# Loading the first four input tiles as row pairs, and moving the V weights to another queue

## The chip, the cores and the metric

The kernel runs on one core of one Trainium2 chip. The metric is the device time of one execution in microseconds, lower is better. A profiled execution also leaves a trace of the instructions of each engine and of each DMA packet. The engines are named PE (TensorE, matrix multiplication), PEld (its weight load), DVE (VectorE), ACT (ScalarE), POOL (GpSimd) and SP (SyncE, which here only issues DMAs). SPq, ACTq and POOLq are the DMA issues of SP, ACT and POOL.

## The reference

The input x has 2048 tokens (rows) of 512 bf16 values. With `xn = layernorm(x)` (no learned scale), the output is `x + A(xn) + B(xn)`.

```python
def _layernorm(x, axis=-1, eps=1e-5):
    return (x - mean) / sqrt(var + eps)
# A: linear attention, 32 heads of 16
q, k, v = split(xn @ wqkv)
phi(t) = concat(softmax(t @ w_phi), softmax(-(t @ w_phi)))      # per head
kv = sum over tokens of phi(k)^T v ; z = sum over tokens of phi(k)
A = (phi(q) kv / (phi(q) z + 1e-6)) @ wo
# B: gated unit, inner width 1792
B = ((xn @ w_gate) * (xn @ w_up)) @ w_down
```

Every step but the sum over tokens in `kv` and `z` works on one token at a time, and that sum does not depend on the order of the tokens.

## The kernel before, in words

The tokens are cut into 16 tiles of 128 rows. `xall` holds all of x in SBUF, tile n at `xall[:, n, :]`, and partition p of tile n is row 128n + p. Four tiles are a group. `xnT` is the normalised x, transposed, so that it can be an operand of every projection.

PE, DVE, ACT, POOL and SP each run their instructions in the order in which the program writes them (`tc.manual_schedule`, line 87); an engine that waits holds up all that stands behind it on that engine.

The start of the program matters here:

- **Loads** (lines 82 to 103). SP issues x tile 0, x tile 2, the second half of `wv` (`dma_wv(2, DC)`, rows 256 to 511 of the V weights), then the first columns of `wg` and `wu`, then `wphi`, more of `wg` and `wu`, a transposing load of the K weights (`wT2`), x tiles 4 to 7, and so on. ACT issues x tile 1 and the first half of `wv`, behind the load of its function table and in front of its other work. POOL issues x tile 3.
- **Semaphores.** The loads by SP and ACT take turns on eight completion semaphores, so a load waits, on the queue that issues it, for the load that had its semaphore eight loads earlier. The load by POOL has a semaphore of its own.
- **Warm-up** (lines 305 to 315). Nine matmuls on constants run on PE while the first tile is under way.
- **First group** (lines 376 to 405). For tiles 0 to 3 the layer norm is folded in later: only the row sum is subtracted before the transposition. `sum_of(0)` sums tile 0 on DVE; ACT sums tiles 1 and 2 (`junk`, line 378, with an accumulated output `tot`); `sum_of(3)` is on DVE. `sub_sum(n)` (line 338, DVE) writes `xns[n]`, `lt(n)` (line 206, PE) transposes it into a PSUM bank and ACT or DVE copies it to `xnT` (line 207). `first_v(n, js)` multiplies `xnT` of tile n by chunks `js` of `wv`: chunks 0 and 1 are the first half, 2 and 3 the second. The order on PE is: tile 0 transposed, tile 1 transposed, `first_v(0, (0, 1))`, tile 2 transposed, `first_v(1, (0, 1))`, `first_v(2, (0, 1))`, `first_v(0, (2, 3))`, tile 3 transposed, and the rest.
- The order on DVE is: sum of tile 0, `sub_sum` of 0 in two halves, `sub_sum` of 1, two copies, `sub_sum` of 2, a copy, sum of tile 3, a copy, `sub_sum` of 3, then the statistics of the four tiles. The order on ACT is: the two sums, then three copies.

After that the program interleaves units of the gated unit (`ffn`, 8 matmuls each) with the projections of K, V and Q, the sums of `kv`, and, in its second half, attention and the output tiles (`fin`). `fin(n)` adds x and stores tile n from SP (line 302). At the end SP waits for the semaphores of all engines and DMAs, one after the other, and all engines meet in a barrier.

Of the kernel before, what the change touches and what calls it, by code (L numbers as in the profile page):

```python
# [21 lines left out]
def kernel(  # L22
# [12 lines left out]
    nc = tc.nc  # L35
    P = 128
# [4 lines left out]
    NT = S // P  # L41
    DC = D // P
# [4 lines left out]
    TT = GT * P  # L47
    E1 = DH + 1

    x_view = A_x.flatten_outer_dims().rearrange("(n p) d -> p n d", n=NT)  # L50
    out_view = out.flatten_outer_dims().rearrange("(n p) d -> p n d", n=NT)

    consts = ctx.enter_context(tc.tile_pool(name="consts", bufs=1))
    wpool = ctx.enter_context(tc.tile_pool(name="wpool", bufs=1))
# [2 lines left out]
    xall = xpool.tile([P, NT, D], BF16)  # L57
# [10 lines left out]
    def dma_x(lo, hi, eng=nc.sync):  # L68
        eng.dma_start(out=xall[:, lo:hi, :], in_=x_view[:, lo:hi, :])

    def dma_cols(eng, w, src, lo, hi, at=0):
        eng.dma_start(out=w[:, :, lo - at:hi - at], in_=src[:, lo:hi].rearrange("(c p) f -> p c f", p=P))

    def dma_wv(lo, hi, eng):
        eng.dma_start(out=wv[:, lo:hi, :],
                      in_=A_wqkv[lo * P:hi * P, 2 * D:3 * D].rearrange("(c p) f -> p c f", p=P))

    def dma_gu(lo, hi):
        dma_cols(nc.sync, wg, B_w_gate, lo, hi)
        dma_cols(nc.sync, wu, B_w_up, lo, hi)  # L80

    dma_x(0, 1)
    dma_x(2, 3)
    dma_wv(2, DC, nc.sync)

    ET = mybir.EngineType
    ctx.enter_context(tc.manual_schedule(engines={ET.PE, ET.DVE, ET.Activation, ET.Pool, ET.SP}))
    ones = nc.const_aps.tensor(1.0, [P, P], BF16)
    first = consts.tile([P, 1], BF16)
    nc.scalar.activation(out=first[:], in_=ones[:, 0:1], func=AF.Exp, scale=1.0)  # L90
    dma_x(1, 2, nc.scalar)
    dma_wv(0, 2, nc.scalar)
    dma_x(3, 4, nc.gpsimd)
    dma_gu(0, 2 * P)
    nc.sync.dma_start(out=wphi[:], in_=A_w_phi.rearrange("(c h) d f -> (h d) c f", c=DC))
    dma_gu(2 * P, 5 * P)
# [49 lines left out]
    def bank(name, dt=F32, n=TT):  # L146
        return ps_s.tile([P, n], dt, name=name, tag="s")
# [137 lines left out]
    def fin(n, cuts=(0, D)):  # L285
        T, t4 = n // GT, n % GT
        for lo, hi in zip(cuts, cuts[1:]):
            w = hi - lo
            ps = bank("fin")[:, 0:w]
            for f in range(FC):  # L290
                nc.tensor.matmul(ps, lhsT=hTs[T][:, f, t4 * P:(t4 + 1) * P], rhs=wd[:, f, lo:lo + w],  # L291
                                 start=(f == 0), stop=False)
            for c in range(DC):
                nc.tensor.matmul(ps, lhsT=oTs[n][:, c, :], rhs=wo[:, c, lo:lo + w],  # L294
                                 start=False, stop=(c == DC - 1))
            o_sb = opool.tile([P, w], BF16, name=f"o_sb{w}")
            if n < GT:
                nc.vector.scalar_tensor_tensor(out=o_sb[:], in0=ps, scalar=r2[n][:], in1=xall[:, n, lo:lo + w],
                                               op0=ALU.mult, op1=ALU.add)
            else:  # L300
                nc.vector.tensor_tensor(out=o_sb[:], in0=ps, in1=xall[:, n, lo:lo + w], op=ALU.add)  # L301
            nc.sync.dma_start(out=out_view[:, n, lo:lo + w], in_=o_sb[:])


    warm = bank("warm")
# [153 lines left out]
    with tc.tile_pool(name="ps_ab", bufs=1, space=PSUM) as ps_ab, \  # L459
# [23 lines left out]
        for n in range(NT):  # L483
            attend(n)
            if n + 5 < NT:
                qproj(n + 5)
            if n < 2:
                ffn(2)
                continue
            fin(n - 2)  # L490
            if n >= 4:
                ffn(2)
        ffn(len(units))
        fin(NT - 2)
        fin(NT - 1, (0, 3 * P, D))


# [28 lines left out]
```

## Time and profile before

| what | us |
|---|---|
| time, median of 3 runs | 220.43 (220.23 to 220.95) |
| time of the profiled execution | 220.46 |
| its span, first to last instruction | 218.8 |
| around the span | 1.66 |
| PE busy in the span | 214.9 |
| DVE busy | 141.0 |
| ACT busy | 89.2 |
| POOL busy | 74.9 |

The span is what the trace shows; 1.66 us of the time lie outside it. A view by line groups the instructions; a view in order of time shows the start, the duration, the engine, the line, the output tile and its input. "Idle before" is how long the engine had nothing to do before that instruction, and the arrow names what ended this.

### The profile page before, as it was taken

What the parts mean: (1) busy time and instruction counts of PE and PEld (TensorE: products, weight loads), DVE (VectorE), ACT (ScalarE), POOL (GpSimd) and SP (SyncE); (2) the same over time, 40 slices, a digit from 0 to 9 for tenths busy, and PEclk for the clock granted to TensorE, in tenths of its full rate; (3) what the DMA queues carried; (4) which work ended last, traced back from release to release, by engine and by line L of the source; (5) the groups of instructions that cost most, each with busy time, mean ns of one, the idle gap of its engine ahead of it and who ended that gap; (6) DMA issues with size and microseconds to landing.
All of it is one profiled execution on the core that took longest, in us unless ns stands there. A gap on an engine that the chain in (4) does not pass through costs nothing.

```text
span 218.8 us, 3493 instructions
## 1 busy us (share of the span) xinstructions
PE 214.9 (98%) x1291; PEld 103.1 (47%) x1291; DVE 141.0 (64%) x242; ACT 89.2 (41%) x159; POOL 74.9 (34%) x72
## 2 busy tenths in 40 slices
PE   8999999999999999999999999999999999999994
PEld 3444445454444444444544444444444444454443
DVE  4878867786598758576599773296655655454321
ACT  5545686569575875565435212141231322100000
POOL 4450843373357554636045333033123033000000
PEclk9999999999999999999999999999999999999999
DMA  5999996005202240202028355114461431412201
GB/s 198 286 297 372 372 219 136 2 0 51 48 0 49 51 94 2 48 3 48 1 43 105 76 114 114 37 24 96 96 70 30 95 72 28 96 48 72 69 30 48
DMA packets 48433, 19.91 MB, mean 91 GB/s; under 512 B 37504, under 2 KB 48384, under 8 KB 48416
## 3 DMA queue, kind: packets, MB, share of 16 engines
q1 hardware_dynamic: 47952, 19.16, 38.9%
q10 hardware_dynamic: 416, 0.39, 0.5%
q8 instruction: 10, 0.16, 0.3%
q0 software_dynamic: 48, 0.13, 0.2%
q14 instruction: 7, 0.06, 0.1%
HBM read 8.67 MB, written 2.10 MB: 49 GB/s over the span
## 4 chain that ended last, share of the span: by engine, by line
PE 97%; DMA 1%; DVE 1%; issue 0%
PE g L275 22%; PE fin L291 22%; PE u L279 22%; PE fin L294 6%; PE q L237 6%; PE k L237 6%; PE pv L237 6%; PE kv L331 2%; PE ab L465 2%; DMA xall<-in_A_x_dram 1%; PE kv L237 1%; PE tp L206 1%; PE pq L226 1%; DVE tot L374 0%; DVE xn L338 0%; DVE o_sb L301 0%
## 5 line engine op out<-in xcount | busy, mean ns | idle before, releaser
L275 PE MATMUL g<-xnT,wg 128*128 128x512 bf16 x224 | 57.5, 379 | 0.0
L279 PE MATMUL u<-xnT,wu 128*128 128x512 bf16 x224 | 57.5, 379 | 0.0
L254 POOL TENSOR_TENSOR phiq<-e,rsum 128x1024 bf16<-128x1024 f32 x16 | 30.9, 1933 | 63.5 <-DVE rsum L252 56.0
L283 DVE TENSOR_TENSOR hT<-u,g_sb 128x512 bf16<-128x512 f32 x56 | 37.0, 666 | 23.9 <-PE u L279 15.8
L282 ACT CAST g_sb<-g 128x512 bf16<-128x512 f32 x56 | 32.9, 587 | 46.8 <-PE g L275 46.5
L250 DVE TENSOR_REDUCE sums<-e 128x64 f32<-128x1024 f32 x32 | 38.9, 1216 | 20.1 <-ACT e L247 20.1
L291 PE MATMUL fin<-wd,hT 128*128 128x512 bf16 (+2 forms) x238 | 51.1, 366 | 0.0
L254 POOL TENSOR_TENSOR phik<-e,rsum 128x1024 bf16<-128x1024 f32 x16 | 30.9, 1932 | 39.6 <-DVE rsum L252 33.6
L279 PEld LDWEIGHTS <-wu 128*128 128x128 bf16 x224 | 21.9, 98 | 26.4
L291 PEld LDWEIGHTS <-hT 128*128 128x128 bf16 x238 | 22.4, 98 | 24.8
L275 PEld LDWEIGHTS <-wg 128*128 128x128 bf16 x224 | 21.1, 98 | 24.0
L237 PEld LDWEIGHTS <-xnT 128*128 128x128 bf16 x192 | 17.4, 98 | 18.2 <-ACT xnT L207 0.7
L301 DVE TENSOR_TENSOR o_sb<-fin,xall 128x512 bf16<-128x512 f32 (+2 forms) x13 | 8.5, 651 | 20.5 <-PE fin L294 20.5
L252 DVE RECIPROCAL rsum<-sums 128x64 f32<-128x64 f32 x32 | 17.7, 553 | 3.1
L294 PE MATMUL fin<-wo,oT 128*128 128x512 bf16 (+2 forms) x68 | 16.6, 366 | 0.0
L237 PE MATMUL k<-W1k,xnT 128*128 128x512 bf16 x64 | 16.4, 379 | 0.0
L237 PE MATMUL q<-W1q,xnT 128*128 128x512 bf16 x64 | 16.4, 378 | 0.0
L246 ACT ACTIVATE e<-q 128x512 f32<-128x512 f32 x12 | 7.2, 597 | 22.2 <-PE q L237 22.2
L237 PE MATMUL pv<-wv,xnT 128*128 128x512 bf16 x56 | 14.4, 379 | 0.0
L478 DVE TENSOR_TENSOR otok<-ab,rden 128x512 bf16<-128x512 f32 x16 | 11.1, 692 | 0.6
L323 ACT CAST vt<-pv 128x512 bf16<-128x512 f32 x12 | 7.0, 587 | 10.0 <-PE pv L237 10.0
L154 DVE BATCH_NORM_STATS2 stats<-xall 128x6 f32<-128x512 bf16 x16 | 10.6, 664 | 0.0
(63 smaller groups left out, 131.8 us busy)
## 6 DMA issues: line engine op xcount, KB each, us to landing
out_dram<-o_sb SPq DMA_DIRECT2D x15, 128.0 KB, 2.0
wd<-in_B_w_down_dram SPq DMA_DIRECT2D x1, 1792.0 KB, 15.8
xall<-in_A_x_dram SPq DMA_DIRECT2D x1, 1024.0 KB, 11.9
wg<-in_B_w_gate_dram SPq DMA_DIRECT2D x1, 640.0 KB, 7.7
wu<-in_B_w_up_dram SPq DMA_DIRECT2D x1, 640.0 KB, 10.4
xall<-in_A_x_dram SPq DMA_DIRECT2D x1, 512.0 KB, 4.5
wg<-in_B_w_gate_dram SPq DMA_DIRECT2D x1, 512.0 KB, 5.3
wu<-in_B_w_up_dram SPq DMA_DIRECT2D x1, 512.0 KB, 6.4
```

The lines of the kernel that those rows point to most:

```text
L154: nc.vector.bn_stats(out=stats[:], in_=xall[:, n, :])
L237: nc.tensor.matmul(ps, lhsT=xnT[:, j, n * P:(n + 1) * P], rhs=w[:, j, :], start=(j == 0), stop=(j == DC - 1))
L250: nc.vector.tensor_reduce(out=sums[:], in_=ev, axis=AX.X, op=ALU.add)
L252: nc.vector.reciprocal(out=rsum[:].rearrange("p a b -> p (a b)"), in_=sums[:])
L254: nc.gpsimd.tensor_tensor(out=phi[:].rearrange("p g (x f) -> p (g x) f", f=DH), in0=ev, in1=rsum[:].to_broadcast((P, 2 * H, DH)), op=ALU.mult)
L275: nc.tensor.matmul(gps, lhsT=wg[:, c, f * P:(f + 1) * P], rhs=xnT[:, c, T * TT:(T + 1) * TT], start=(c == 0), stop=(c == DC - 1))
L279: nc.tensor.matmul(ups, lhsT=wu[:, c, f * P:(f + 1) * P], rhs=xnT[:, c, T * TT:(T + 1) * TT], start=(c == 0), stop=(c == DC - 1))
L282: nc.scalar.copy(out=g_sb[:], in_=gps)
L283: nc.vector.tensor_tensor(out=hTs[T][:, f, :], in0=ups, in1=g_sb[:], op=ALU.mult)
L291: nc.tensor.matmul(ps, lhsT=hTs[T][:, f, t4 * P:(t4 + 1) * P], rhs=wd[:, f, lo:lo + w], start=(f == 0), stop=False)
L294: nc.tensor.matmul(ps, lhsT=oTs[n][:, c, :], rhs=wo[:, c, lo:lo + w], start=False, stop=(c == DC - 1))
L478: nc.vector.tensor_tensor(out=o_tok[:].rearrange("p (b h d) -> p b h d", b=2, d=DH), in0=abv[:, :, :, 0:DH], in1=rden[:].to_broadcast((P, ...
```

## The change

Tiles 0 and 1 become a pair, and tiles 2 and 3 as well. A pair is 256 consecutive rows of x. Partition p gets rows 2p and 2p + 1 of these 256, the first in the even tile's slot of `xall` and the second in the odd tile's slot. The two rows lie next to each other in memory and in the partition, so a pair is one load of 128 pieces of 2 KB, where there were two loads of 128 pieces of 1 KB each. Each of the four tiles then holds other rows than before, and the store of tiles 0 to 3 goes by the same map. SP issues both pairs; ACT issues the two halves of `wv`; POOL issues no load. There is one load less by SP and ACT, and one less by POOL.

```diff
+    PAIRS = (0, 2)
+    def pair(rows, n):
+        return rows[n * P:(n + 2) * P, :].rearrange("(p j) d -> p j d", j=2)
+    def out_of(n, lo, hi):
+        if n // 2 * 2 in PAIRS:
+            return pair(out_rows, n // 2 * 2)[:, n % 2, lo:hi]
+        return out_view[:, n, lo:hi]
...
+    def dma_pair(n, eng=nc.sync):
+        eng.dma_start(out=xall[:, n:n + 2, :], in_=pair(x_rows, n))
...
-    dma_x(0, 1)
-    dma_x(2, 3)
-    dma_wv(2, DC, nc.sync)
+    dma_pair(0)
+    dma_pair(2)
...
     nc.scalar.activation(out=first[:], in_=ones[:, 0:1], func=AF.Exp, scale=1.0)
-    dma_x(1, 2, nc.scalar)
     dma_wv(0, 2, nc.scalar)
-    dma_x(3, 4, nc.gpsimd)
+    dma_wv(2, DC, nc.scalar)
     dma_gu(0, 2 * P)
...
-            nc.sync.dma_start(out=out_view[:, n, lo:lo + w], in_=o_sb[:])
+            nc.sync.dma_start(out=out_of(n, lo, lo + w), in_=o_sb[:])
```

More of the change, by code (lines that the diff above doesn't have):

```diff
@@ L48 @@
     E1 = DH + 1
-    x_view = A_x.flatten_outer_dims().rearrange("(n p) d -> p n d", n=NT)
-    out_view = out.flatten_outer_dims().rearrange("(n p) d -> p n d", n=NT)
+    x_rows, out_rows = A_x.flatten_outer_dims(), out.flatten_outer_dims()
+    x_view = x_rows.rearrange("(n p) d -> p n d", n=NT)
+    out_view = out_rows.rearrange("(n p) d -> p n d", n=NT)
+    PAIRS = (0, 2)
[5 more added lines that the diff above has]
+        return out_view[:, n, lo:hi]
     consts = ctx.enter_context(tc.tile_pool(name="consts", bufs=1))
```

## The prediction

> **What bounds the kernel now.** I read the page first (busy shares and the chain that ended last), then the chain in order of time, the DMA issues, and the instructions of the first 10 us.
>
> ```profile
> span 218.8 us, 3493 instructions
> ...
> PE 214.9 (98%) x1291; PEld 103.1 (47%) x1291; DVE 141.0 (64%) x242; ACT 89.2 (41%) x159; POOL 74.9 (34%) x72
> ...
> PE 97%; DMA 1%; DVE 1%; issue 0%
> ```
>
> PE is the bound: 97% of the chain. No later wait of DVE, ACT or POOL is on it, so the change can act at two places only: before PE's stream begins, and after it ends.
>
> ```profile
> 0.79 2.45 DMA xall<-in_A_x_dram
> ...
> 3.27 0.70 DVE tot L374
> ...
> 3.99 0.30 DVE xn L338
> ...
> 4.34 1.07 PE tp L206 x8
> 5.40 0.54 PE kv L237 x2
> 5.94 0.22 PE tp L206 x4
> ```
>
> The chain in order of time (start, duration): x tile 0 lands at 0.79 + 2.45 = 3.24, DVE sums and subtracts, and PE starts at 4.34. By the starts of its matmuls PE then has about 0.1 us of holes from 5.56 to 9.34, so what delays it there delays the end one to one.
>
> ```profile
> xall<-in_A_x_dram SPq DMA_DIRECT2D x2, 128.0 KB, 2.6
> wv<-in_A_wqkv_dram ACTq DMA_DIRECT2D x1, 256.0 KB, 3.4
> wv<-in_A_wqkv_dram SPq DMA_DIRECT2D x1, 256.0 KB, 4.4
> ...
> xall<-in_A_x_dram ACTq DMA_DIRECT2D x1, 128.0 KB, 2.7
> xall<-in_A_x_dram POOLq DMA_DIRECT2D x1, 128.0 KB, 4.1
> ```
>
> The last number is from issue to landing. With the issue times of the trace and its records of single packets and landings (x0 0.79, x1 0.85, x2 1.25, first half of wv 1.28, x3 1.29, second half 1.71) the pieces land at 3.25, 3.55, 3.91, 4.64, 5.41 and 6.15. The packets of SP and ACT flow nearly in the order of issue, whatever the queue: those of the second wv half, issued at 1.71, begin at 4.25, when ACT's queue is empty.
>
> ```profile
> 3.57 0.63 ACT L378 ACTIVATE junk<-xall 128x512 bf16<-128x512 bf16 x1 [1.28 <-DMA xall<-in_A_x_dram]
> ...
> 4.33 0.63 ACT L378 ACTIVATE junk<-xall 128x512 bf16<-128x512 bf16 x1
> ...
> 4.86 0.19 ACT L378 ACTIVATION_READ_ACCUMULATOR junk<-xall 128x1 f32 x1
> ...
> 5.19 0.34 DVE L338 TENSOR_SCALAR xn<-xall,tot 128x512 bf16<-128x512 bf16 x1
> ...
> 5.65 0.68 DVE L374 TENSOR_REDUCE tot<-xall 128x1 f32<-128x512 bf16 x1
> ...
> 7.39 0.39 PE L206 MATMUL tp<-ident,xn 128*128 128x128 bf16 x4
> ```
>
> Instructions in order of time: the second sum on ACT (tile 2) starts at 4.33 with no wait, because tile 2 landed at 3.91. Its result, 0.72 us later at 5.05, is what `sub_sum` of tile 2 needs on DVE at 5.19. That is the margin which the change touches.
>
> **The change, part by part.** The sum is made against the profiled execution: 220.46 us, a span of 218.8 and 1.66 around it; it stands 0.03 over the median of 220.43.
>
> Landing of the pairs. Pieces flow in the order of issue, so I count bytes. Before, 256 KB (x0, x1) were in by 3.55, 384 KB by 3.91, 640 KB by 4.64: 256 KB take 0.73. After, the order is pair 0 (SP 0.79), first wv half (ACT 0.85), pair 2 (SP about 1.2), second half (ACT about 1.3). Pair 0 is the first 256 KB: 3.55. Pair 2 ends the first 768 KB: 3.55 + 2 x 0.73 = 5.01. A 2 KB packet is not in this trace; packets of 512, 768, 1024 and 1280 bytes take 27, 39, 46 and 58 ns, which extends to an estimate of 84 to 94 ns, against 92 for two of 1 KB. A tenth of two pairs is 0.15, so I take 4.9. The ends: pair 0 at 3.25, as tile 0 alone now, or at 3.9, if half of its time is shared with wv; pair 2 at 4.28 (before the wv half) or at 5.7 (1 MB, behind both halves: 3.55 + 3 x 0.73).
>
> Tile 0 and 1. DVE's sum starts 0.30 later (3.57). Tile 1 lands at 3.55 in both, so ACT's first sum keeps its time and is not waited for. `sub_sum` of tile 1 ends 0.30 later, PE transposes tile 1 from 5.10 to 5.53, and its two matmuls with wv take 0.43 at the spacing of 0.216 seen from 6.0 on (before, 5.20 to 5.78, the first at 0.36). PE would be free for tile 2 at 5.96, against 5.78: +0.19, not +0.30, since two slow matmuls become fast.
>
> Tile 2. ACT's second sum waits for pair 2: 4.9 + 0.02 to 5.64, with the read 0.19 behind, 0.85 in all after landing as measured from the first sum's landing to its release. `sub_sum` of 2 starts at 4.9 + 0.87 = 5.77 (it could have at 5.49), and PE transposes 0.40 later (sub_sum 0.34, 0.06 to the matmul): 6.17 against 5.775, **+0.40**. Behind this wait stand, on ACT, the copies of tiles 1 and 2 and, on DVE, a copy, the sum of tile 3, a copy, and `sub_sum` of 3. The latter moves by 0.58, from 6.44 to 7.02, and ends at 7.36; PE wants tile 3 at 7.39 + 0.40 = 7.79. It is covered by 0.43. Tile 3 is there with tile 2. So the front loses 0.40, between 0 (pair 2 by 4.3, pair 0 at 3.25) and 1.2 (pair 2 at 5.7: 6.97 against 5.775).
>
> The wv halves. The first lands at about 4.3 (512 KB) and is wanted at 5.5; the second at about 5.6 (1 MB), wanted at 7.0 + 0.4. No cost; the cover would be gone at a delay of 1.2 and 1.8.
>
> Issues. SP loses one issue of 0.43, so wg and wu go out 0.47 earlier; wg landed at 7.08 and is wanted at 9.3. The transposing load of the K weights now waits for pair 2 instead of the second wv half (6.15) and goes out perhaps 0.7 earlier; PE needs it at 14.6 and is never idle for it by more than 0.1. The third pair of gate columns waits for nothing, the third of wu for pair 0. POOL loses 0.77 of issue, ahead of the identity matrix (ready at 2.65, wanted at 4.34) and of masks used at 12.6: nothing. ACT's two issues stay two, in front of a table load that ends at 2.07. DVE loses one semaphore wait. Stores of tiles 0 to 3 keep 128 pieces of 1 KB, in the middle of the run: 2.0 us to landing, and nobody waits.
>
> The end. The last store lands at 217.72. SP waits for it in the third of six two-semaphore steps, and then walks through 217.75, 217.82, 217.88 and 217.94 to the barrier: 0.06 each. As the semaphores now fall, the last store is in the last of five steps, so three steps behind it go: **-0.18** (0 if each step waited anyway, -0.2 at most).
>
> Sum: +0.40 - 0.18 = +0.22. Span 219.0, time 220.46 + 0.22 = **220.7**.
>
> The clock. The 512-column warm-up matmuls stand 0.427 apart, those from 6.0 on 0.216; the change falls at 5.48, 4.65 us after the first warm-up. Before, PE idles from 3.99 to 4.34; after, to 4.64. I take the clock to rise at the same place.
> The Trainium skill ("TensorE: Matmul & The Clock Gate", Part 1) says that the clock is released after a window of about 3.4 us that was busy enough, windows that run freely; the spacing here agrees, and by it a failed window would cost an estimated half of 3.4, 1.7 us, for a time near 222.4.
> For pair 0, the packets seen go by order of issue. The Trainium skill ("DMA: Bandwidth & Descriptors", Queues, rings and completion order) says that a DMA engine takes turns between queues packet by packet; by that pair 0 would share with wv and land near 3.9, sub_sum of 2 could start at 5.84, and the sum would be 220.8.
>
> **The rivals.**
> 1. Pair 2 behind both wv halves, slower. The second wv half before waited 2.5 us from issue to first packet behind ACT's queue; if SP's second load is held up likewise until ACT's 512 KB are through, pair 2 lands at 5.7, the front loses 1.2 and the time is 220.46 + 1.2 - 0.18 = 221.5. It decides from a landing of 5.4 on (each 0.1 later is 0.1 at the end). Against it: tile 2, issued just before the first wv half, came before it.
> 2. The clock falls back, slower. The longer hole makes PE's time so thin that the release starts anew with the first transposition: 4.64 + 4.65 = 9.3 instead of 5.48, and PE does half in these 3.8 us: +1.9, 222.6. For it: the hole doubles to 0.65. Against: PE ran for 3.2 us before.
> 3. The pairs come early: with 2 KB pieces and no POOL packets, pair 0 at 3.25 and pair 2 by 4.3. The front loses nothing, the end gains 0.18: 220.3. Against: 12 of 16 DMA engines start only at 2.4, and 0.7 of packets and 0.3 to the semaphore follow.
> 4. The part outside the span shrinks because POOL no longer uses a DMA queue. This part is 1.66 us, so the gain lies between 0 and 1.66; at 1.0 the time is 219.7. It decides from 0.9 on. Nothing in the trace speaks for it, and POOL's first and last instructions stay as they are.
>
> **How the numbers follow.** 0.3% is 0.66 us, about what this kernel's runs can tell from no change (they spread by 0.72). Chances: forecast 0.52, including the shared pair 0 of 220.8; rival 1 0.17; rival 2 0.10; rival 3 0.13; rival 4 0.08. The range 220.1 to 221.7 leaves out rivals 2 and 4, 0.18. The forecast's own range is 220.4 to 221.0. Faster by over 0.3% (under 219.8): rival 4 and some scatter, 0.10. Within: forecast and rival 3 less scatter, 0.62. Slower (over 221.1): rivals 1 and 2 and a little of the forecast, 0.28.
>
> **What would show it.** The chain begins with pair 0, landing near 3.55; ACT's second sum starts near 4.9 after a wait for the DMA; PE transposes tile 2 at 6.17 and starts the first gate matmul at 9.34 + 0.40 = 9.74; the step from 0.427 to 0.216 stays near 5.5; the last store's landing is followed by the barrier within 0.13. I am wrong if ACT does not wait for pair 2, if it waits beyond 5.4, or if matmuls past 6 us stand 0.427 apart.

## The result, and the profile after

The changed kernel takes 221.03 us (median of 22 runs, 220.87 to 222.81) against 220.69 us (220.17 to 221.10) for the kernel before in runs beside it: the ratio is 1.0023, with a 95% interval of 1.0014 to 1.0032. The ratio goes by the means (221.12 against 220.61, 0.51 us apart), and one run of 222.81 pulls on them; the medians lie 0.34 us apart. So the change makes the kernel slower, by 0.15 to 0.23 percent. The profiled execution took 221.12 us, 0.66 more than that of before.

The page of the changed kernel: span and instructions, busy times, and the shares of the chain that ended last by engine.

```profile
span 219.4 us, 3489 instructions
...
PE 215.4 (98%) x1291; PEld 103.0 (47%) x1291; DVE 141.1 (64%) x242; ACT 89.0 (41%) x159; POOL 74.1 (34%) x71
...
PE 97%; DMA 1%; DVE 1%; issue 0%
```

PE is still 97% of the chain. From the first gate matmul to the last matmul of the program both traces have 206.34 us (9.338 to 215.676 before, 10.178 to 216.516 after). So the whole of the change lies in front of the first gate matmul, which comes 0.84 later, and behind the last matmul. The first gate matmuls in order of time, first of the kernel before, then of the changed kernel:

```profile
9.34 1.03 PE L275 MATMUL g<-xnT,wg 128*128 128x512 bf16 x4
...
10.18 1.03 PE L286 MATMUL g<-xnT,wg 128*128 128x512 bf16 x4
```

The chain of the changed kernel in order of time (start, duration, what), up to tile 2:

```profile
0.79 2.77 DMA xall<-in_A_x_dram
...
3.59 0.70 DVE tot L385
...
4.31 0.30 DVE xn L349
...
4.65 1.07 PE tp L217 x8
5.72 0.85 PE kv L248 x2
...
6.61 0.40 PE tp L217 x4
7.00 0.43 PE kv L248 x2
```

Pair 0 lands at 3.56, PE starts at 4.65 instead of 4.34, and the four transpositions of tile 2 stand at 6.61, where they stood at 5.78 in the kernel before:

```profile
5.78 0.39 PE L206 MATMUL tp<-ident,xn 128*128 128x128 bf16 x4
```

What held them in the changed kernel is in its instructions in order of time (start, duration, engine, line, what; in brackets the idle time before and what ended it):

```profile
3.58 0.63 ACT L389 ACTIVATE junk<-xall 128x512 bf16<-128x512 bf16 x1 [1.30 <-DMA xall<-in_A_x_dram]
...
5.44 0.63 ACT L389 ACTIVATE junk<-xall 128x512 bf16<-128x512 bf16 x1 [1.13 <-DMA xall<-in_A_x_dram]
...
6.19 0.35 DVE L349 TENSOR_SCALAR xn<-xall,tot 128x512 bf16<-128x512 bf16 x1 [0.60 <-ACT junk L389]
...
6.60 0.23 PEld L217 LDWEIGHTS <-xn 128*128 128x128 bf16 x4 [0.93 <-DVE xn L349]
```

ACT's second sum, which started at 4.33 without a wait, now waits 1.13 for the DMA; DVE waits 0.60 for ACT, and PE's weight load waits 0.93 for DVE. That is the chain of three engines behind pair 2.

The DMA issues of the changed kernel (count, size of each, time from issue to landing):

```profile
xall<-in_A_x_dram SPq DMA_DIRECT2D x2, 256.0 KB, 3.4
wv<-in_A_wqkv_dram ACTq DMA_DIRECT2D x2, 256.0 KB, 4.3
```

The trace's landings are 3.56 for pair 0, 4.68 for the first wv half, 5.35 for pair 2 and 6.11 for the second half: the order of issue. After the last matmul the changed kernel gains: its last store lands at 218.54 (before 217.70), SP reaches the closing barrier 0.14 later (before 0.31), and the barrier takes 0.69 (before 0.755). Together 0.23 comes off. These times are read from the records of the landings and of SP's closing waits. The span grows by 0.84 - 0.23 = 0.61.

### The profile page after: what moved, and what is told of

It is laid out like the page before. It is cut to its first block, busy times and chain, and to the rows that moved or that the text cites. A ratio compares the mean times of both kernels' runs of the same rounds, so it can differ in the third digit from the quotient of the medians.

```text
span 219.4 us, 3489 instructions
## 1 busy us (share of the span) xinstructions
PE 215.4 (98%) x1291; PEld 103.0 (47%) x1291; DVE 141.1 (64%) x242; ACT 89.0 (41%) x159; POOL 74.1 (34%) x71
## 4 chain that ended last, share of the span: by engine, by line
PE 97%; DMA 1%; DVE 1%; issue 0%
PE g L286 22%; PE fin L302 22%; PE u L290 22%; PE fin L305 6%; PE k L248 6%; PE q L248 6%; PE pv L248 6%; PE kv L342 2%; PE ab L476 2%; DMA xall<-in_A_x_dram 1%; PE kv L248 1%; PE tp L217 1%; PE pq L237 1%; DVE tot L385 0%; DVE xn L349 0%; DVE o_sb L312 0%
```

## The experiments

**Both wv halves behind the pairs, on SP.**

```diff
     dma_pair(0)
     dma_pair(2)
+    dma_wv(0, 2, nc.sync)
+    dma_wv(2, DC, nc.sync)
...
-    dma_wv(0, 2, nc.scalar)
-    dma_wv(2, DC, nc.scalar)
```

> The changed kernel with both halves of wv issued by SyncE behind the two pairs; ScalarE issues nothing. Theory (pair 2 is late because the first wv half, issued 0.4 us ahead of it from the other queue, goes first): pair 2 now ends the first 512 KB and lands near 4.3 instead of 5.35, sub_sum of tile 2 starts at 5.5 instead of 6.19, tile 2 is transposed near 6.0 instead of 6.6 and the time falls by about 0.6, to 220.4. The first wv half lands near 5.1 and is wanted at 5.6. Rival (a 2 KB pair that is second on its queue is slow whatever stands beside it): pair 2 stays near 5.3 and the time near 221.0.

Measured: 220.85 us (12 runs), ratio to the kernel before 1.0018 (0.9997 to 1.0039). Pair 2 lands at 4.24, and the chain of three engines is gone. Instructions in order of time of this variant:

```profile
4.39 0.63 ACT L389 ACTIVATE junk<-xall 128x512 bf16<-128x512 bf16 x1
...
5.56 0.34 DVE L349 TENSOR_SCALAR xn<-xall,tot 128x512 bf16<-128x512 bf16 x1
...
5.75 0.59 PE L248 MATMUL kv<-wv,xnT 128*128 128x512 bf16 x2 [0.16 <-DMA wv<-in_A_wqkv_dram]
...
6.18 0.39 PE L217 MATMUL tp<-ident,xn 128*128 128x128 bf16 x4
```

ACT's second sum follows the first without a wait. In place of that wait PE now waits 0.16 for the first wv half, which lands at 5.71, not 5.1. The first gate matmul comes at 9.75, 0.43 earlier than in the changed kernel. So what was issued ahead of pair 2 made it late, not the pair itself; but the median is only 0.18 under that of the changed kernel, not 0.6, since wv became the next to be late. Two of the 12 runs, at 222.60 and 222.71, are far above the others (the last section comes back to such runs).

**Pair 2 issued by ACT.**

```diff
     dma_pair(0)
-    dma_pair(2)
...
+    dma_pair(2, nc.scalar)
     dma_wv(0, 2, nc.scalar)
```

> The changed kernel with pair 2 issued by ScalarE, ahead of the two wv halves; SyncE issues pair 0 and then wg. Theory (order of issue decides): pair 2 ends the first 512 KB and lands near 4.3, and the time falls by about 0.5, to 220.5; pair 0 stays at 3.55. Rival (queues share packet by packet): pair 0 moves to 3.9 to 4.2, both pairs end together near 4.3, PE starts its transpositions 0.4 to 0.6 later than in the changed kernel and the time falls by only 0.2.

Measured: 221.47 us (11 runs), ratio 1.0055 (1.0035 to 1.0075). The DMA issues of this variant:

```profile
wv<-in_A_wqkv_dram ACTq DMA_DIRECT2D x2, 256.0 KB, 5.5
...
xall<-in_A_x_dram SPq DMA_DIRECT2D x1, 256.0 KB, 3.2
xall<-in_A_x_dram ACTq DMA_DIRECT2D x1, 256.0 KB, 3.5
```

Pair 2 lands at 4.34, as order of issue has it, but pair 0 at 3.99: here two loads issued 0.06 apart share, as the rival said. And the first wv half, issued at 1.27, lands only at 6.12: by the packet records, the first gate columns, issued by SP at 1.25, start 280 of their packets from 3.75 to 4.25, where the wv half starts 11, and from 4.25 on the packets of the two queues share the time. Neither expectation had the time right, which rose instead of falling. The first transposition is at 5.08. In the profiled execution PE's clock also rose late, at 8.73 (below), which makes its first gate matmul, at 11.30, no measure of the landings alone.

**The changed queues without the pairs.** The edit is against the kernel before.

```diff
     dma_x(0, 1)
+    dma_x(1, 2)
     dma_x(2, 3)
-    dma_wv(2, DC, nc.sync)
+    dma_x(3, 4)
...
-    dma_x(1, 2, nc.scalar)
     dma_wv(0, 2, nc.scalar)
-    dma_x(3, 4, nc.gpsimd)
+    dma_wv(2, DC, nc.scalar)
```

> The kernel before with x tiles 0, 1, 2, 3 each issued by SyncE (128 KB, 1 KB pieces, in this order) and both wv halves by ScalarE: the changed queues without the pairs. Theory (order of issue and bytes): tile 0 lands at 3.25, the first wv half goes next, tile 1 lands near 4.4, the second wv half next, tiles 2 and 3 near 5.7 to 6.1; sub_sum of tile 2 starts near 6.8 and the time is about 221.6, slower than the changed kernel by 0.6. Rival (the 2 KB pieces are what costs): tile 2 lands before 4.9 and the time is 220.5, that of the kernel before.

Measured: 222.62 us (10 runs), ratio 1.0080 (1.0052 to 1.0108). Tile 0 lands at 2.95, the first wv half at 3.87, tile 1 at 4.19, tile 2 at 5.88, tile 3 at 6.48, the second wv half at 6.13. The four shortest runs are at 221.28 to 221.38, 0.4 over the shortest of the changed kernel; tile 2 lands 0.53 later than pair 2 does there. So the 2 KB pieces are not what costs, and order and bytes hold but for one pair of loads: the second wv half, issued at 1.31, lands after tile 2, issued at 1.71. The other six runs are at 222.46 to 223.62. For three of them, 223.29 (the profiled one) to 223.62, the granted clock over the span was 0.992, where it was 0.998 to 1.0 in all other runs; what held the other three is not shown. A table by stretches of this variant: from and to, length, busy time and count of PE, PEld, DVE, ACT and POOL, granted clock of PE, DMA share, GB/s.

```profile
3.55:6.90 3.35, 1.68 (x13) 0.67 (x11) 1.52 (x7) 1.66 (x5) 0.00 (x0) 1.00 1.07 317
6.95:10.30 3.35, 3.17 (x12) 1.49 (x13) 3.28 (x10) 0.37 (x1) 0.90 (x3) 0.50 1.31 274
10.40:13.00 2.60, 2.60 (x16) 1.14 (x14) 1.94 (x6) 1.86 (x3) 2.13 (x6) 1.00 0.99 194
```

The clock was at full speed, PE was busy for only half of the next 3.4 us, and then it ran at 0.50 for a stretch and rose again. The longest single gap between two of its matmuls in that time was about 1.1 us. The entries of the clock in the trace are at 3.506, 6.919 and 10.332: exactly 3.413 apart.

**One load more, to move the last semaphore.**

```diff
-    nc.sync.dma_start(out=wphi[:], in_=...)
+    nc.sync.dma_start(out=wphi[:, 0:2, :], in_=...)
+    nc.sync.dma_start(out=wphi[:, 2:DC, :], in_=...)
```

> The changed kernel with wphi in two loads instead of one, so that one more load takes its turn on the eight semaphores and the last store's semaphore is waited for in the third of the five last steps instead of the fifth. Theory (part of the gain at the end is the place of that wait): front as in the changed kernel, 0.12 more between the last store's landing and the barrier (0.26 instead of 0.14), span and time longer by 0.1. Rival (the gain at the end comes from having no load by GpSimd): 0.14 as in the changed kernel, time 221.0.

Measured: 221.27 us (12 runs), ratio 1.0041 (1.0017 to 1.0065). Between the landing of the last store and the barrier 0.249 pass, not 0.140; the barrier takes 0.698, as in the changed kernel. So of the 0.23 gained at the end, 0.11 is the place of the last store's wait among SP's closing steps, and 0.06 is the step that went (six to five). The other 0.06, in the barrier, goes with POOL's load: all ten kernels without one have 0.69 to 0.705, the two kernels with one 0.755 and 0.749. The times alone would not show this: the median is 0.24 over that of the changed kernel, not 0.1, three of the 12 runs are at 222.84 to 222.92, and the profiled span is no longer (219.3), since pair 2 landed at 5.21 in it.

**Less of wv ahead of pair 2.**

```diff
-    dma_wv(0, 2, nc.scalar)
+    dma_wv(0, 1, nc.scalar)
+    dma_wv(1, 2, nc.scalar)
```

> The changed kernel with the first wv half in two loads of 128 KB on ScalarE instead of one of 256 KB, so that only a quarter of wv is issued ahead of pair 2. Theory (pair 2 waits for what is issued ahead of it): pair 2 lands between 4.3 and 4.9 instead of 5.35, tile 2 is transposed near 6.05 instead of 6.6, and the time falls by 0.4 less the 0.1 that one more load costs at the end, to 220.7. Rival (all that ScalarE issues goes ahead of SyncE's second load): pair 2 stays near 5.3, time 221.1.

Measured: 222.05 us (12 runs), ratio 1.0057 (1.0034 to 1.0079); the profiled execution took 220.85. In it pair 2 lands at 5.01, a little later than expected, and the first gate matmul stands at 9.84, 0.34 earlier than in the changed kernel. Pair 0, however, lands at 3.92, beside the quarter of wv at 4.08: here the two queues did share. PE's hole up to the first transposition, 0.67 in the changed kernel, grows to about 1.1 us, and 5 of the 12 runs are above 222.1. The landing of pair 2 moved the way the theory says; the median is spoiled by something else. I take it to be the clock, which the next two runs look into with the changed kernel; a fill was not tried on this variant.

**A shorter and a longer warm-up.**

The shorter one, against the changed kernel:

```diff
-    warm_up(7)
-    warm_up(2, 1)
+    warm_up(6)
```

The longer one:

```diff
     warm_up(7)
-    warm_up(2, 1)
+    warm_up(8, 1)
```

> The changed kernel with six warm-up matmuls of 512 columns instead of seven and two short ones, so that PE's hole before the first transposition is 1.3 us instead of 0.67. Theory (PE's clock rises at the end of a window of 3.41 us that held enough work, and windows lie anywhere in a run): in more of the runs the window fails, and those take 1.6 us more; the shortest runs stay at 220.9, at least 4 of 12 lie above 222.3. Rival (the runs near 222.8 have another cause): at most 1 of 12 above 222.3.

> The changed kernel with six more warm-up matmuls of 128 columns (0.64 us), which fill PE's hole up to the first transposition. Theory (window of work): none of the runs above 222.3, median 220.9 to 221.0, since the wait for pair 2 sets the rest. Rival: as the changed kernel, a run above 222.3 in 10 or 20; or the first transposition starts late behind the fill and the median goes up by 0.1 or more.

Measured, shorter: 221.74 us (12 runs), ratio 1.0046 (1.0030 to 1.0063). Three runs are at 220.78 to 220.82, eight at 221.5 to 222.0 and one at 222.51, so one above 222.3 where at least four were expected. By that count alone the rival would have it; but nine of the 12 runs lie 0.7 or more above the other three, so most runs do pay, 0.7 to 1.2 and not 1.6. In the profiled execution the clock rose at 8.18, and the matmuls before that show it. PE of this variant, in order of time:

```profile
4.80 1.06 PE L217 MATMUL tp<-ident,xn 128*128 128x128 bf16 x8 [1.26 <-DVE xn L348]
5.66 1.06 PE L248 MATMUL kv<-wv,xnT 128*128 128x512 bf16 x2
6.51 0.63 PE L217 MATMUL tp<-ident,xn 128*128 128x128 bf16 x4
6.94 1.06 PE L248 MATMUL kv<-wv,xnT 128*128 128x512 bf16 x2
```

Two matmuls of 512 columns take 1.06 at 6.94, where the changed kernel's took 0.59 at 6.84. From the landing of pair 2 (5.11) to the first gate matmul (10.80) 5.69 us pass, 0.87 more than in the changed kernel. That the price is smaller than 1.6 fits with part of the slow work lying beside the wait for pair 2.

Measured, longer: 220.81 us (12 runs, 220.77 to 220.97), ratio 1.0009 (1.0000 to 1.0018). No run is above 221. The clock rose at 3.94 in the profiled execution, and the first gate matmul is at 9.99. This is the tightest set of runs of all, and its median is 0.2 under that of the changed kernel (whose ratio was 1.0023): the fill costs nothing, as the first transposition waits 0.45 for DVE anyway. That the fill gains the 0.2 is less firm, since the intervals of the two ratios overlap (1.0014 to 1.0032 for the changed kernel), and with a chance of 1 in 22, as the changed kernel had, 12 runs without one above 222.1 would be no surprise either.

**Only tiles 2 and 3 as a pair.**

```diff
-    PAIRS = (0, 2)
+    PAIRS = (2,)
...
-    dma_pair(0)
+    dma_x(0, 1)
     dma_pair(2)
+    dma_wv(2, DC, nc.sync)
...
+    dma_x(1, 2, nc.scalar)
     dma_wv(0, 2, nc.scalar)
-    dma_wv(2, DC, nc.scalar)
```

> The kernel before with tiles 2 and 3 as a pair from SyncE in the place of tile 2, and no load by GpSimd: SyncE issues tile 0, pair 2 and the second wv half, ScalarE tile 1 and the first wv half. Theory (what is issued ahead of pair 2 decides, the pairs cost nothing by themselves): tile 0 lands at 3.25 and tile 1 at 3.55 as in the kernel before, pair 2 ends the first 512 KB near 4.25, in time for ScalarE's second sum at 4.33; the front keeps the time of the kernel before (first gate matmul at 9.34) and the end keeps half of its gain, so the time is 220.5, 0.2 under the kernel before. Rival (2 KB pieces or the missing GpSimd load slow the start): first gate matmul near 10, time 221.0.

Measured: 220.49 us (12 runs, 220.21 to 220.86), against 220.62 for the kernel before in the same set, ratio 0.9997 (0.9987 to 1.0008). ACT's two sums of this variant:

```profile
3.62 0.63 ACT L390 ACTIVATE junk<-xall 128x512 bf16<-128x512 bf16 x1 [1.34 <-DMA xall<-in_A_x_dram]
...
4.61 0.63 ACT L390 ACTIVATE junk<-xall 128x512 bf16<-128x512 bf16 x1 [0.26 <-DMA xall<-in_A_x_dram]
```

With 256 KB ahead of it on the two queues, pair 2 lands at 4.52 and ACT waits 0.26 instead of 1.13. The first gate matmul is at 9.50. So pair 2 from SP and no load by POOL cost nothing that can be measured in the time, which came out as expected although pair 2 landed 0.27 later than that. Together with the variant that has wv behind the pairs this puts the cost on the wv half ahead of pair 2; what pair 0 would cost by itself no run separates, as tile 0 is alone again here. It is the lowest median of all the variants, but it can't be told from the kernel before.

**The kernel before and this variant, with a fill.**

```diff
-    warm_up(2, 1)
+    warm_up(5, 1)
```

> The kernel before with three more warm-up matmuls of 128 columns, which fill most of PE's hole of 0.35 us up to the first transposition. Theory (the spread of the kernel before, 220.15 to 221.2, is the place of the clock's rise in the front, which has no wait to absorb it): the window holds enough work in more runs, the longest runs fall to 220.9 or less and the median by 0.1 to 0.2, to 220.5. Rival (the spread is in the landing of tile 0): median 220.65 and the same spread.

> The variant with tiles 0 and 1 as before and pair 2 from SyncE, with the same three more warm-up matmuls. Theory (front of the kernel before, half of the gain at the end, an earlier clock): median 220.35, under both kernels. Rival: 220.5 as without the fill.

Measured: 220.72 us (220.31 to 221.21), ratio 1.0002 (0.9990 to 1.0013), and 220.53 us (220.25 to 221.18), ratio 0.9996 (0.9985 to 1.0006). Neither has gained, and the spread of the kernel before stays. My theory of that spread fell: filling its hole of 0.35 changed neither the median nor the spread. The second one shows what may: its pair 2 landed at 5.02 and its first wv half at 5.58, where the same loads without the fill, issued within 0.01 of the same times, landed at 4.52 and 5.02. Landings of the same loads move by half a microsecond between executions. That they make up the whole spread was not shown.

**Across the runs.** The landing of pair 2 (or tile 2) against the first gate matmul, in us from the start of the span:

| kernel | landing | first gate matmul | difference |
|---|---|---|---|
| changed | 5.35 | 10.18 | 4.83 |
| wphi in two | 5.21 | 10.04 | 4.83 |
| longer warm-up | 5.16 | 9.99 | 4.83 |
| wv quarters | 5.01 | 9.84 | 4.83 |
| pair 2 alone, filled | 5.02 | 9.85 | 4.83 |
| pair 2 alone | 4.52 | 9.50 | 4.98 |
| before, filled | 4.06 | 9.21 | 5.15 |
| wv behind the pairs | 4.24 | 9.75 | 5.51 |
| before | 3.91 | 9.34 | 5.43 |

The three kernels left out had the clock down for a part of this stretch (shorter warm-up 5.69, pair 2 by ACT 6.97, the queues without the pairs 6.28). Wherever pair 2 lands at 5.0 or later and the clock is up, the end follows at a fixed distance: one to one. In the profiles with a landing of 4.52 or earlier the distance is longer, so something else decides there: the first wv half in the variant with wv behind the pairs, and by my reading the slow matmuls and the chain of tile 0 in the others.

## Why the prediction was right, and where it was off

**The place.** Right: PE is the bound, nothing changed between the first gate matmul and the last matmul (206.34 in both), and the change acts through ACT's second sum, `sub_sum` of tile 2 on DVE and the transposition of tile 2.

**The landing of pair 0.** Forecast 3.55, measured 3.56, with the sum of tile 0 starting at 3.59 for 3.57 and PE starting at 4.65. That is nearer than the method deserves: the three other profiles with the same loads have pair 0 at 3.61, 3.71 and 3.84.

**The landing of pair 2.** This is the term that was mis-sized: forecast 4.9, measured 5.35. Counting bytes at 256 KB per 0.73 gave the right order of the pieces but not the time of the first wv half: forecast 4.3, it landed at 4.68, 1.12 after pair 0. Pair 2 came 0.67 after that, about as reckoned (its 2 KB packets took 84 ns, the low end of the estimate), and the second half 0.76 later. The half was issued 0.44 earlier than before (0.84 for 1.28), behind 256 KB instead of 384 KB, and landed as late as before (4.64). By the packet records 50 to 62 of its packets start in each quarter microsecond from 3.0 to 4.0, where 85 to 89 of them did before from 3.5 to 4.0. The DMA engines were not full at that time. Here is the stretch from 3.00 to 3.75, first of the kernel before, then of the changed kernel, in the same columns as the table by stretches above (DMA share is the last but one and can pass 1, as packets overlap; the column of the clock reads 1.00 where a trace has no entry yet):

```profile
3.00:3.75 0.75, 0.75 (x3) 0.21 (x2) 0.48 (x1) 0.18 (x1) 0.63 (x2) 1.00 1.06 365
...
3.00:3.75 0.75, 0.75 (x3) 0.21 (x2) 0.16 (x1) 0.17 (x1) 0.00 (x0) 1.00 0.84 251
```

At 251 instead of 365 GB/s some 86 KB less move in this stretch, which at 256 KB per 0.73 is an estimated 0.24 us, about half of what pair 2 was late. Why the packets came so slowly is not settled. The three other profiles with the same loads ahead of pair 2 have it at 5.21, 5.16 and 5.11, so the size of the error is 0.2 to 0.45. The prediction named an ACT that waits beyond 5.4 as a sign of being wrong, and a landing from 5.4 on as what decides for its first rival. In the profiled execution ACT's second sum starts at 5.44 and pair 2 lands at 5.35, so it stands on that edge; in the three others the sum starts at 5.30, 5.25 and 5.19. The landing between the two wv halves is still the order that was forecast.

**The front.** Forecast +0.40 (between 0 and 1.2), measured +0.84 in the profiled pair: 0.45 from that landing, the rest as reckoned. The steps behind it had the right distances: `sub_sum` of tile 2 came 0.84 after the landing (0.87 forecast) and PE 0.41 after that (0.40). Tile 3 and both wv halves were covered, as said.

**The clock.** I took it to rise at the same place. It did not: in the changed kernel the matmuls at 5.51 and 5.94 still stood 0.427 apart, and the next ones, at 6.6, were fast. Two matmuls that I had counted fast were slow; it cost nothing beside the wait for pair 2, as they were over at about 6.4. The trace of the changed kernel has no entry of the granted clock; the spacing of the matmuls is what shows the rise.

**The end.** Forecast -0.18, measured -0.23: the three steps behind the last store's wait are gone (0.31 to 0.14), and the barrier lost 0.06 with POOL's load, which I had not counted. (The 217.72 of the prediction is the end of SP's wait; the store itself landed at 217.70.)

**The sum.** Forecast +0.22 against the profiled execution. Measured +0.66 between the two profiled executions and +0.34 between the medians; the first pair has an early execution of before (220.46 with a median of 220.69) and the latest of the four landings of pair 2. The time, 221.03, lies in the range, 0.33 over the point and just over the forecast's own 220.4 to 221.0, and the change stays within 0.3%, the case given most. Of the 0.33 about 0.2 is the base: I added to one execution at 220.46, where the median of before turned out as 220.69. That the change in the medians, 0.34, is so near to 0.22 is partly luck, as the front of the profiled pair was off by 0.44.

**The rivals.** Pair 2 behind both wv halves: no, it came between them (4.68, 5.35, 6.11). The pairs early: no. Time outside the span: 1.66 before, 1.72 after (221.12 less 219.4), no gain. The clock: a late rise is real (8.18 and 8.73 in two variants), but not as the rival has it, in every run. One run of the changed kernel of 22 is at 222.81, 1.8 over the median; it has no trace, so that the clock made it so is likely and not shown; of the 112 runs of the kernel before in four sets one is at 222.34 and none other above 221.3.
The Trainium skill ("DMA: Bandwidth & Descriptors", Queues, rings and completion order) has DMA engines take turns between queues packet by packet, and a packet there is typically 9 to 17 descriptors, drained whole before the turn. If the pieces are spread evenly over the 16 engines and each is a descriptor, a pair has 8 on each engine and a wv half 16 (an estimate), so that rule need not make two loads alternate piece by piece, as my estimate of 3.9 took it. The landings show both: pair 0 at 3.56 to 3.84 in the four profiles with the same loads, and 3.99 beside pair 2 from ACT and 3.92 beside a quarter of wv. By the packet records 1 packet of wv starts before 3.0 in the changed kernel, and 24 in the variant with quarters. So the rule alone did not tell the landing.

## What to carry to other kernels

When the bound engine runs without holes, look at the first microseconds for the one operand that is already just in time, and ask of every load what is issued ahead of it on any queue, not on its own alone: a load moved up on one queue pushed back the second load of the other. Merging two loads made the first tile as late as the second here (3.56 for 3.25). And count what stands behind the last store's wait: which semaphore it gets can be worth a tenth of a microsecond, for no work at all.

## What the runs showed of the hardware that was not expected

In the one trace with more than one change of PE's clock the entries lie 3.413 us apart, and where the first rise falls differs from run to run: in the 11 profiles that have an entry it rose at 3.51, 3.73, 3.94, 4.15, 4.46, 4.89, 5.28, 5.48, 5.73, 8.18 and 8.73. From the matmuls' starts one can reckon how much of the 3.41 us before such a moment PE was busy, if the moments keep that distance. By this the two rises at 8.18 and 8.73 came a window late: their windows before (1.35 to 4.76 and 1.90 to 5.31) were busy for about 58% and 67%. The least busy windows that ended in a rise were busy for about 78% and 77% (0.09 to 3.51, and 1.86 to 5.28), and one that was busy for 50% (3.51 to 6.92 in the queues without the pairs) ended in a fall. So in these profiles the bound lies between 67% and 77%. This mostly fits who is hit: with the hole of 0.35 of the kernel before 1 run of 112 is above 222.1, with about 0.7 in the kernels with both pairs 1 of 22, 3 of 12 and 2 of 12, with 1.1 in two variants 5 of 12 and 5 of 11, with the longer warm-up 0 of 12. The shorter warm-up, with the longest hole, has only 1 of 12 there, though 9 of 12 above 221.5. Single runs have no trace, so their clock is inferred.
The Trainium skill ("TensorE: Matmul & The Clock Gate", Part 1) states free-running windows of 3413 ns; the entries 3.413 apart agree to the nanosecond.

Loads that are the same and issued at the same times landed up to 0.5 us apart between two executions (pair 2 at 4.52 and 5.02), which is more than the whole difference of the two kernels. Single profiles of such a start have to be read in several copies.
